# One inversion pass over 62 slots for two disjoint token lists, in place of two passes

## The chip, the cores and the metric

The kernel runs on one core of a Trainium2 chip. The metric is the device time of one execution, in microseconds; where there are several runs, their median.

## The reference, cut to what matters

A causal seven-tap convolution along the sequence is followed by two mixtures of eight experts. The first one is skipped by tokens whose skip score isn't positive, and adds its result to its input; the second one takes every token.

```python
def reference(x, weight, moe, moe2):
    x = conv(x, softmax(weight)).reshape(N, D)      # N = 14336, D = 192, F = 1024, E = 8
    do = x @ moe.w_skip > 0
    xc = x[do]
    e, gate = argmax(xc @ moe.w_gate), max(softmax(xc @ moe.w_gate))
    x[do] = xc + gate * (relu(xc @ moe.w1[e]) @ moe.w2[e])
    logits = x @ moe2.w_gate + moe2.modality_bias[modality_id]
    e, gate = argmax(logits), max(softmax(logits))
    return gate * (relu(x @ moe2.w1[e]) @ moe2.w2[e])
```

## The kernel before, in words

**Stages.** Phase 1 convolves all tokens in 8 groups of 16 columns of 112 tokens, computes the gates of both mixtures, and writes a row for each token to DRAM (`rows`). The tokens then go through the experts in *jobs*: a job is a list of up to 128 row numbers (one slot, 128 tokens) and one expert. `Ffn.run` goes over the jobs: it gathers a job's rows by an indirect DMA on GpSimd, transposes them by DMA, multiplies with w1 (`mm1`, two halves of 20 matmuls; relu on ScalarE into `hh`, remainder on VectorE into `hlo`), and one job later with w2 (`mm2`), whose result VectorE and ScalarE scale with `c`.

**Jobs in order.** 56 jobs of the first mixture from fixed slots (7 per expert), 6 jobs of the tokens that overflow these slots (list `l1`, `NS1` = 6), 56 jobs of the second mixture for tokens that skip the first (list `lb`, `NS2B` = 56, the first 54 as pairs with one expert), and 58 jobs of the second mixture for the others, whose codes the first mixture's results give (list `l2`). The two lists `l1` and `lb` are made while the first 56 jobs run.

**How a list is made.** `route` has two halves. The *placement* (`ranks` and what follows it) gives every token of the list a position: one-hot codes `rA`, a running count `rC` over 128x1024 elements, two small TensorE products on the counts `cnt`, slot bounds `se`, per-expert shifts (`rB`, `rC`; 16 instructions, only for the paired list), a masking and a sum to `pos` (128x128, zero for a token that isn't in the list). It also makes the table `tab` of experts per slot, from which the weight loads read, and `nrem`, the count of slots that didn't fit. The *inversion* (`qsl`, `invert`) turns positions into row numbers per slot. `qsl` splits `pos` into a place `q` and a slot `sl`. `invert` goes over the 128 token columns in 16 chunks of 8: VectorE compares an iota with `q` into `oa` (128x1024) and with `sl` into `ob` (128 x 8S), multiplies `ob` by the row number, and TensorE adds up 8 products of `oa` and `ob`, S columns each, in one PSUM bank. S is 6 for `l1` and 56 for `lb`. `finish` writes the row numbers as `idx` (for `l1`) and `idxB` (for `lb`).

**What sets the order.** The instructions of VectorE, ScalarE, TensorE and GpSimd run in the order in which the program issues them (`InOrder`, whose line 70 is the line of nearly every instruction in the profile). Side work is written as generators. `Tasks.tick` goes one step in each live generator, and `bg` ticks at four points of each job, so a generator's steps lie between the jobs' instructions; a `yield n` skips n ticks. `routes` is such a generator: it waits for the slots of phase 1 (`idxs`), then runs `route` for `l1`, and then `route` for `lb`. Beside it run the two weight-preparation lanes (`prep`: load an expert's weights, a Gram product on TensorE with `dg` and `ssq` on VectorE and a small product with `ones`, then splits into f16 parts on ScalarE, GpSimd and VectorE, and stores) and `scale2` on finished results (`mx`, `s`, `ef`). At job 56 `bg` drains all that is left of them.

**What waits for the lists.** `run` gathers a job up to four jobs ahead (five for a pair) if its list is `ready`, and `need` steps `routes` until the list is there when the job is two ahead. The weights of overflow and second-mixture jobs are loaded on SP's queue, up to nine jobs ahead, as soon as `tab` is there and their buffer (one of three) is free.

Of the kernel before, what the change touches and what calls it, by code (L numbers as in the profile page):

```python
# [7 lines left out]
F32 = mybir.dt.float32  # L8
# [4 lines left out]
ALU = mybir.AluOpType  # L13
# [11 lines left out]
NT = 128  # L25
# [17 lines left out]
NS1 = 6  # L43
NP2B, NS2B = 27, 56
# [70 lines left out]
class Moe:  # L115
# [258 lines left out]
    def route_a(self, g, code, pool, ob, res):  # L374
        nc = self.nc
        S = NSA
        acc = self.acc[0][:, (g % 2) * S:(g % 2) * S + S]
        if g == 0:
# [5 lines left out]
        def count(h):  # L384
            a, b = AB.pop(h)
            for t in range(8):
                nc.tensor.matmul(acc, a[:, :, t], b[:, :S, t], start=(h % 2 == 0 and t == 0), stop=(h % 2 == 1 and t == 7))

# [53 lines left out]
        for h in (2 * g, 2 * g + 1):  # L442
# [5 lines left out]
            yield 2  # L448
            nc.vector.tensor_tensor(b[:, :S], self.iq[:, :S], sl[:, u].unsqueeze(1).to_broadcast([128, S, 8]), ALU.is_equal)
            nc.vector.tensor_tensor(b[:, :S], b[:, :S], self.val[:, u].unsqueeze(1).to_broadcast([128, S, 8]), ALU.mult)  # L450
            yield 2
# [4 lines left out]
        yield 2  # L456
        t1 = pool.tile([128, S], F32, name="t1a")
        nc.vector.tensor_scalar(t1, acc, 0.0, 2048.0 * g, ALU.is_gt, ALU.mult)
# [104 lines left out]
        yield 1  # L563

    def route(self, code, nst, tag, pool, ob, res, base=0, lag=1, S=None, np=0, lp=None, val=None):
        nc = self.nc
        lp = lp or self.cp
        S = S or nst
        T = code.shape[-1]
        r = []  # L570
        for w in self.ranks(code, pool, 1, r):
# [39 lines left out]
            yield 1  # L611
        nc.vector.tensor_tensor(cum, cum, oh, ALU.mult)
        yield 1
        pos = pool.tile([128, T], F32, name="pos")
        nc.vector.tensor_reduce(pos, cum.rearrange("p c t -> p t c"), AX.X, ALU.add)
        yield 1
        q, sl = self.qsl(pos, pool)
        yield 1
        ef = ob.tile([128, S + 6], F32, name="esl", bufs=1)
        nc.vector.memset(ef[:, 0:6], -1.0)  # L620
# [7 lines left out]
        tab = lp.tile([128, S, 2], I32, name="tab" + tag)  # L628
# [11 lines left out]
            nc.vector.tensor_tensor(tab[:, :, 1], ef[:, 6:], ef[:, 3:S + 3], ALU.not_equal)  # L640
        nrem = res.get("nrem") or lp.tile([128, 1], I32, name="nrem" + tag)
        nc.vector.tensor_scalar(nrem, se[:, 1 if np else 0, 8:9], -float(nst), 0.0, ALU.add, ALU.max)
        res.update(tab=tab, nrem=nrem)
        yield 1
        for w in self.invert(S, q, sl, pool, ob, tag, res, lp, lag, base, val):
            yield w


class Phase1:
# [454 lines left out]
def build(tc, x, cw, m1w1, m1w2, mod, bias2, m2w1, m2w2, wgs, out):  # L1104
    with ExitStack() as ctx:
        m = Moe(tc, ctx)
        nc = m.nc
# [6 lines left out]
        rt = ctx.enter_context(tc.tile_pool(name="rt", bufs=1))  # L1114
        ob = m.oa = ctx.enter_context(tc.tile_pool(name="ob", bufs=4))
        pw = ctx.enter_context(tc.tile_pool(name="pw", bufs=2))
        pq = ctx.enter_context(tc.tile_pool(name="pq", bufs=4))
        la, ls, l1, lb, l2, lr = {}, {}, {}, {}, {}, {}
# [35 lines left out]
        def routes():  # L1154
            while "idx" not in ls:
                yield 1
            va = m.cp.tile([128, NSA], F32, name="va")
            ra["va"] = va
            k = 0
            while k < NSA:  # L1160
                c = order[k][0] * SB + order[k][1]
                n = 1
                while k + n < NSA and order[k + n][0] * SB + order[k + n][1] == c + n:
                    n += 1
                nc.gpsimd.tensor_copy(va[:, k:k + n], ls["va"][:, c:c + n])
                k += n
                yield 1
            for i in m.route(m.code[:, 0, :], NS1, "1", rt, ob, l1, lag=2):
                yield i
            for i in m.route(m.code[:, 1, :], NS2B, "B", rt, ob, lb, lag=2, np=NP2B):  # L1170
                yield i

        tk, tk2, tkw = Tasks(), Tasks(), Tasks()
# [29 lines left out]
        w = {}  # L1203

        def late_pools():
            st.close()
            m.py.append(m.py2)
            m.ph.append(m.ph3)
            px = ctx.enter_context(tc.tile_pool(name="px", bufs=1))
            w["x"] = px.tile([128, NC - XA, D], F32, name="x2s")  # L1210
            po = sp.enter_context(tc.tile_pool(name="po", bufs=1))
            pw2 = sp.enter_context(tc.tile_pool(name="pw2", bufs=2))
            w["pw2"] = pw2
            tkw.add(lane(1))
            o = po.tile([128, 4, F], F16, name="o1"), po.tile([128, W2C + 2], F16, name="o2")
            w["o"] = o
            tk.add(routes())
# [44 lines left out]
        n1, n2 = NC, NC + NS2B  # L1262
# [110 lines left out]
```

## Time and profile before

| | us |
|---|---|
| three runs, median (lowest to highest) | 1087.74 (1078.09 to 1090.42) |
| the profiled execution | 1090.2 |
| its span, first to last instruction | 1088.4 |
| TensorE busy | 983.2 (90%) |
| VectorE busy | 696.8 (64%) |
| ScalarE busy | 492.7 (45%) |
| GpSimd busy | 626.7 (58%) |
| mean granted clock | 0.935 |

In the profile PE is TensorE's matmuls, PEld its weight loads, DVE VectorE, ACT ScalarE, POOL GpSimd, and SP the queue that issues most DMAs. Busy shares are averages over stages with different limits; a matmul's own duration is longer than its distance to the next, since matmuls are pipelined. The granted clock is a share of full speed: 1.00 is 2.4 GHz, 0.50 is 1.2 GHz, and values between are means over a stretch with both. Most instructions are issued through a helper and show its line, L70, so they are told apart by the names of their tiles. The two lists are made between 233 and 519 us of the span.

### The profile page before, as it was taken

To read this page: it belongs to the slowest core of one execution; us is meant where nothing else is said; L and a number is where in the kernel's file an instruction comes from. 1 tells how busy PE (TensorE), PEld (TensorE's weight loads), DVE (VectorE), ACT (ScalarE), POOL (GpSimd) and SP (SyncE) were. 2 spreads that over 40 slices of the span, in tenths; PEclk is the share of its full clock that TensorE was granted. 3 is DMA by queue.
4 is the path that set the end of the run, shared out by engine and by line. 5 is a ranking of instruction groups with operands and counts; after the bars stand their busy time and mean duration, and the time that the engine had idled before them with its cause. 6 is when DMAs were issued, how large, how long until landed. Compare 5 with 4: busy or idle time off the path is not lost.

```text
span 1088.4 us, 27310 instructions
## 1 busy us (share of the span) xinstructions
PE 983.2 (90%) x10104; PEld 818.9 (75%) x10104; DVE 696.8 (64%) x1813; ACT 492.7 (45%) x903; POOL 626.7 (58%) x1110
## 2 busy tenths in 40 slices
PE   6788988899999779999889999999997999999993
PEld 4566767778888668888777777788786888888882
DVE  4386876679998889888446666667753444444441
ACT  3374643443755635455345555553233333334331
POOL 4054667777756836676437777774434555555531
PEclk9897765999999888999999999999999999999997
DMA  5666446675679737867963333443156332323330
GB/s 197 210 227 236 132 148 215 159 225 162 188 183 278 217 124 224 242 203 222 286 225 98 94 105 92 106 102 90 49 141 242 80 74 71 78 72 71 79 118 15
DMA packets 109134, 165.35 MB, mean 152 GB/s; under 512 B 80975, under 2 KB 86073, under 8 KB 103232
## 3 DMA queue, kind: packets, MB, share of 16 engines
q1 hardware_dynamic: 94368, 134.02, 39.6%
q0 software_dynamic: 13920, 28.87, 11.3%
q8 instruction: 81, 1.33, 0.5%
q10 hardware_dynamic: 704, 0.63, 0.2%
q14 instruction: 61, 0.50, 0.1%
HBM read 181.56 MB, written 58.42 MB: 220 GB/s over the span
## 4 chain that ended last, share of the span: by engine, by line
PE 57%; DVE 16%; DMA 8%; issue 5%; ACT 5%; POOL 5%; SPq 1%; POOLq 0%; ACTq 0%; DVEq 0%
PE bank L70 57%; DVE hlo L70 3%; DMA out_dram<-u,si 3%; DMA ws<-in_moe_w_dram 2%; DVE rC L70 1%; ACT ws L70 1%; DVE ob L70 1%; DVE o L70 1%; ACT hh L70 1%; DVE ws L70 1%; DMA w1b<-s1b 1%; DVE mx L70 1%; DMA gt<-rows,idx 1%; DVE oa L70 1%; DMA gt<-rows,idxB 1%
## 5 line engine op out<-in xcount | busy, mean ns | idle before, releaser
L70 PEld LDWEIGHTS <-w1b 128*128 128x128 f16 x4840 | 374.7, 100 | 54.4 <-issue 13.5
L70 PE MATMUL bank<-xp,w1b 128*128 128x256 f16 x2200 | 266.8, 275 | 9.4 <-DMA w1b<-s1b 4.6
L70 PEld LDWEIGHTS <-ws 128*128 128x128 f16 (+2 forms) x2208 | 192.7, 101 | 67.2 <-DMA ws<-in_moe_w_dram 9.6
L70 PE MATMUL bank<-w2b,ws 128*128 128x384 f16 x1760 | 237.3, 286 | 0.7 <-issue 0.7
L70 DVE SCALAR_TENSOR_TENSOR ws<-bank,ws 128x512 f16<-128x512 f32 x220 | 151.5, 690 | 126.7 <-ACT ws L70 106.6
L70 POOL DMA_INDIRECT out_dram<-u,si x114 | 115.6, 1014 | 188.5 <-DVE u L70 52.1
L70 ACT ACTIVATE ws<-bank 128x512 f16<-128x512 f32 x220 | 130.7, 597 | 118.7 <-PE bank L70 105.9
L70 PE MATMUL bank<-xt,w1b 128*128 128x128 f16 x2640 | 168.9, 224 | 9.1 <-DVE hlo L70 7.0
L70 PE MATMUL bank<-w2b,hh 128*128 128x384 f16 x528 | 142.1, 336 | 2.2 <-DMA w2b<-s2a 1.2
L70 PE MATMUL bank<-w2b,hlo 128*128 128x192 f16 x528 | 131.9, 251 | 0.0
L70 ACT ACTIVATE u<-bank,c 128x192 f32<-128x192 f32 x114 | 48.0, 421 | 156.0 <-PE bank L70 117.2
L70 DVE SCALAR_TENSOR_TENSOR hlo<-bank,hh 128x512 f16<-128x512 f32 x132 | 90.2, 685 | 42.3 <-ACT hh L70 39.0
L70 DVE SCALAR_TENSOR_TENSOR u<-bank,c,u 128x192 f32<-128x192 f32 x114 | 47.6, 418 | 103.3 <-ACT u L70 79.4
L70 ACT ACTIVATE hh<-bank 128x512 f16<-128x512 f32 x132 | 76.2, 593 | 41.6 <-PE bank L70 39.6
L70 ACT COPY xt<-bank 128x384 f16<-128x384 f16 (+1 forms) x110 | 64.0, 582 | 47.9 <-PE bank L70 46.1
L70 PEld LDWEIGHTS <-xt 128*112 128x112 f16 (+1 forms) x570 | 49.1, 138 | 39.9 <-issue 29.8
L70 PEld LDWEIGHTS <-hh 128*128 128x128 f16 x528 | 53.6, 102 | 32.0 <-issue 4.1
L70 POOL DMA_INDIRECT gt<-rows,idx x64 | 63.8, 996 | 11.3 <-issue 9.1
L70 PE MATMUL bank<-xg,band 128*112 128x384 f32 x128 | 63.9, 591 | 0.3 <-DVE s L70 0.3
L70 POOL TENSOR_TENSOR x2s<-x2s,xs 128x192 f32<-128x192 f32 x46 | 31.6, 687 | 54.8 <-DVE x2s L70 45.0
L70 POOL DMA_INDIRECT gt<-rows,idxB x56 | 56.1, 1002 | 12.0 <-issue 7.2
L70 PE MATMUL bank<-g,xt 128*112 128x34 f16 (+1 forms) x570 | 47.3, 199 | 12.0 <-DVE L L70 5.0
(249 smaller groups left out, 1447.4 us busy)
## 6 DMA issues: line engine op xcount, KB each, us to landing
w1b<-s1b SPq DMA_DIRECT2D x59, 1024.0 KB
w2b<-s2b SPq DMA_DIRECT2D x59, 768.5 KB
ws<-in_moe_w_dram SPq DMA_DIRECT2D x16, 768.0 KB
rows<-hl SPq DMA_DIRECT2D x8, 1386.0 KB
xg<-in_x_dram SPq DMA_DIRECT2D x7, 1536.0 KB
ws<-in_moe_w_dram SPq DMA_DIRECT2D x16, 512.0 KB
ws<-in_moe_w_dram SPq DMA_DIRECT2D x32, 256.0 KB
s1a<-w1b SPq DMA_DIRECT2D x8, 1024.0 KB
```

What stands on the lines that cost most here:

```text
L70: r = f(*args, **kw)
```

## The change

`route` is cut in two: `place` (placement, table and `nrem`) and the inversion behind it. The new `route2` places the first list, places the second list, and inverts both at once. A token is in at most one of the two lists, since a token that skips the first mixture isn't among its overflow, so the two position arrays are merged in one: `keep` is the first list's position where it lies within its 6 slots (else zero), and a token of the second list gets its own position plus 6 x 128 (`far` is that shift). One `qsl` and one `invert` over 62 slots follow, and the two lists are slices of the result (`idx1B`). `pos` gets two buffers. `route`, which makes the other lists, does what it did.

```diff
--- before.py
+++ after.py
@@ -563,9 +563,38 @@
         yield 1
 
     def route(self, code, nst, tag, pool, ob, res, base=0, lag=1, S=None, np=0, lp=None, val=None):
+        S = S or nst
+        for w in self.place(code, nst, tag, pool, ob, res, lag, S, np, lp):
+            yield w
+        q, sl = self.qsl(res["pos"], pool)
+        yield 1
+        for w in self.invert(S, q, sl, pool, ob, tag, res, lp, lag, base, val):
+            yield w
+
+    def route2(self, codes, nsts, tags, pool, ob, ress, np, lag):
+        nc = self.nc
+        (c1, cb), (n1, nb), (t1, tb), (r1, rb) = codes, nsts, tags, ress
+        for w in self.place(c1, n1, t1, pool, ob, r1, lag, n1):
+            yield w
+        keep = pool.tile([128, NT], F32, name="keep")
+        nc.vector.scalar_tensor_tensor(keep, r1["pos"], float(n1 * 128), r1["pos"], ALU.is_le, ALU.mult)
+        for w in self.place(cb, nb, tb, pool, ob, rb, lag, nb, np):
+            yield w
+        far = pool.tile([128, NT], F32, name="pos", bufs=2)
+        nc.vector.tensor_scalar(far, rb["pos"], 0.0, float(n1 * 128), ALU.is_gt, ALU.mult)
+        nc.vector.tensor_tensor(keep, keep, far, ALU.add)
+        nc.vector.tensor_tensor(keep, keep, rb["pos"], ALU.add)
+        q, sl = self.qsl(keep, pool)
+        yield 1
+        res = {}
+        for w in self.invert(n1 + nb, q, sl, pool, ob, t1 + tb, res, None, lag):
+            yield w
+        for r, a, b in ((r1, 0, n1), (rb, n1, n1 + nb)):
+            r.update(idx=res["idx"][:, a:b], va=res["va"][:, a:b])
+
+    def place(self, code, nst, tag, pool, ob, res, lag, S, np=0, lp=None):
         nc = self.nc
         lp = lp or self.cp
-        S = S or nst
         T = code.shape[-1]
         r = []
         for w in self.ranks(code, pool, 1, r):
@@ -611,10 +640,8 @@
             yield 1
         nc.vector.tensor_tensor(cum, cum, oh, ALU.mult)
         yield 1
-        pos = pool.tile([128, T], F32, name="pos")
+        pos = pool.tile([128, T], F32, name="pos", bufs=2)
         nc.vector.tensor_reduce(pos, cum.rearrange("p c t -> p t c"), AX.X, ALU.add)
-        yield 1
-        q, sl = self.qsl(pos, pool)
         yield 1
         ef = ob.tile([128, S + 6], F32, name="esl", bufs=1)
         nc.vector.memset(ef[:, 0:6], -1.0)
@@ -640,10 +667,8 @@
             nc.vector.tensor_tensor(tab[:, :, 1], ef[:, 6:], ef[:, 3:S + 3], ALU.not_equal)
         nrem = res.get("nrem") or lp.tile([128, 1], I32, name="nrem" + tag)
         nc.vector.tensor_scalar(nrem, se[:, 1 if np else 0, 8:9], -float(nst), 0.0, ALU.add, ALU.max)
-        res.update(tab=tab, nrem=nrem)
-        yield 1
-        for w in self.invert(S, q, sl, pool, ob, tag, res, lp, lag, base, val):
-            yield w
+        res.update(tab=tab, nrem=nrem, pos=pos)
+        yield 1
 
 
 class Phase1:
@@ -1165,9 +1190,7 @@
                 nc.gpsimd.tensor_copy(va[:, k:k + n], ls["va"][:, c:c + n])
                 k += n
                 yield 1
-            for i in m.route(m.code[:, 0, :], NS1, "1", rt, ob, l1, lag=2):
-                yield i
-            for i in m.route(m.code[:, 1, :], NS2B, "B", rt, ob, lb, lag=2, np=NP2B):
+            for i in m.route2((m.code[:, 0, :], m.code[:, 1, :]), (NS1, NS2B), ("1", "B"), rt, ob, (l1, lb), NP2B, 2):
                 yield i
 
         tk, tk2, tkw = Tasks(), Tasks(), Tasks()
```

VectorE, in the first jobs behind the first placement. Ahead of the change; `oa` and `ob` are the first chunks of the six-slot pass, `hlo`, `c` and `x2a` belong to jobs, `dg` and `ssq` to weight preparation:

```order
L70 SCALAR_TENSOR_TENSOR hlo<-bank_59,hh 128x512
L70 TENSOR_SCALAR esl<-esl 128x6
L70 CAST tab_3803<-esl 128x6
L70 TENSOR_TENSOR tab_3803<-esl 128x6
L70 TENSOR_SCALAR nrem_3807<-se 128x1
L70 TENSOR_TENSOR c<-gt,w2b_79 128x1
L70 TENSOR_TENSOR oa<-iq,q 128x1024
L70 SCALAR_TENSOR_TENSOR x2a<-bank_64,c,x2a 128x192
L70 TENSOR_TENSOR ob<-iq,sl 128x48
L70 SCALAR_TENSOR_TENSOR hlo<-bank_63,hh 128x512
L70 SCALAR_TENSOR_TENSOR hlo<-bank_58,hh 128x512
L70 TENSOR_TENSOR ob<-ob,val 128x48
```

And in the changed program, at the same place:

```order
L70 CAST tab_3770<-esl 128x6
L70 TENSOR_TENSOR tab_3770<-esl 128x6
L70 TENSOR_SCALAR nrem_3774<-se 128x1
L70 SCALAR_TENSOR_TENSOR hlo<-bank_59,hh 128x512
L70 SCALAR_TENSOR_TENSOR keep<-pos 128x128
L70 TENSOR_TENSOR rA<-code,c_205 128x1024
L70 TENSOR_TENSOR c<-gt,w2b_79 128x1
L70 SCALAR_TENSOR_TENSOR rC<-rA 128x1024
L70 MEMSET gend 128x1
L70 COPY gend<-rC 128x8
L70 TENSOR_TENSOR cnt<-gend 128x8
L70 SCALAR_TENSOR_TENSOR x2a<-bank_64,c,x2a 128x192
```

Where the first chunks stood, the second list's placement begins (`rA`, the scan `rC`, `gend`, `cnt`).

VectorE in the changed program, at the end of the second placement (`pos` on the left of the third row is `far`, `x2s` and `mx` belong to jobs):

```order
L70 TENSOR_SCALAR nremB<-se 128x1
L70 TENSOR_REDUCE mx<-x2a 128x4
L70 SCALAR_TENSOR_TENSOR x2s<-bank_60,c,x2s 128x192
L70 TENSOR_SCALAR pos<-pos 128x128
L70 TENSOR_TENSOR keep<-keep,pos 128x128 x2
L70 TENSOR_SCALAR pi<-keep 128x128
L70 TENSOR_SCALAR si<-pi 128x128
L70 TENSOR_SCALAR sl<-si 128x128
L70 TENSOR_SCALAR pi<-pi 128x128
```

The merging stands there, and one `qsl` behind it; in the program before each placement had a `qsl` of its own.

VectorE at the end of the second list's inversion, before the change (`c`, written once per job, has been written 56 times there):

```order
L70 TENSOR_TENSOR rC<-rC,bank_61 128x224
L70 SCALAR_TENSOR_TENSOR x2s<-bank_64,c,x2s 128x192
L70 TENSOR_REDUCE ei_8542<-rC 128x56
L70 TENSOR_TENSOR ei<-ei,ei_8542 128x56
L70 TENSOR_SCALAR vaB<-ei 128x56
L70 TENSOR_SCALAR idxB<-ei 128x56
L70 SCALAR_TENSOR_TENSOR hlo<-bank_58,hh 128x512
```

And at the end of the joint inversion in the changed program (`c` has been written 36 times):

```order
L70 SCALAR_TENSOR_TENSOR hlo<-bank_58,hh 128x512
L70 TENSOR_REDUCE ei_6489<-rC 128x62
L70 TENSOR_TENSOR ei<-ei,ei_6489 128x62
L70 TENSOR_SCALAR va1B<-ei 128x62
L70 TENSOR_SCALAR idx1B<-ei 128x62
L70 TENSOR_SCALAR wsc<-bank_65 128x2
L70 TENSOR_SCALAR wsc<-wsc 128x2 x2
```

The end of the list work has moved ahead by 20 jobs; the list that the overflow jobs read is written there too, where it was written after 31 jobs.

## Rows read from the trace of the kernel before

**Rows 1.** Busy time by stretch of the list work; number of instructions in brackets.

```profile
core 0: us, PE busy (x) PEld busy (x) DVE busy (x) ACT busy (x) POOL busy (x), PEclk, DMA share, GB/s
233.10:259.20 26.10, 24.63 (x332) 21.26 (x331) 22.88 (x48) 11.28 (x18) 21.60 (x30) 1.00 0.67 218
259.20:287.40 28.20, 27.02 (x373) 23.86 (x370) 25.60 (x71) 17.00 (x29) 18.96 (x28) 1.00 0.39 98
259.20:367.60 108.40, 102.19 (x1388) 89.89 (x1386) 96.22 (x239) 66.72 (x118) 74.37 (x108) 1.00 0.70 195
367.60:409.50 41.90, 29.01 (x323) 24.83 (x322) 35.62 (x88) 16.23 (x30) 22.18 (x31) 0.81 0.55 160
409.50:516.40 106.90, 104.64 (x1313) 92.57 (x1312) 93.43 (x216) 59.22 (x106) 74.53 (x107) 0.98 0.74 224
516.40:547.00 30.60, 23.41 (x286) 20.16 (x284) 12.83 (x33) 9.79 (x20) 14.36 (x28) 0.94 0.98 267
```

**Rows 2.** The same stretches, instructions that touch `c` alone; ACT's count is jobs.

```profile
233.10:259.20 26.10, 4.18 (x10) 1.68 (x4) 0.00 (x0) 1.00 0.67 218
259.20:287.40 28.20, 3.64 (x13) 2.52 (x6) 0.00 (x0) 1.00 0.39 98
259.20:367.60 108.40, 12.81 (x41) 8.35 (x20) 0.00 (x0) 1.00 0.70 195
367.60:409.50 41.90, 4.40 (x12) 2.08 (x5) 0.00 (x0) 0.81 0.55 160
409.50:516.40 106.90, 11.98 (x40) 8.34 (x20) 0.00 (x0) 0.98 0.74 224
516.40:547.00 30.60, 3.90 (x12) 2.50 (x6) 0.00 (x0) 0.94 0.98 267
```

**Rows 3.** TensorE in order of time: start, duration; a chunk of each inversion, and what follows.

```profile
268.12 0.61 PE L70 MATMUL bank<-ob,oa 128*128 128x6 f16 x8
268.59 0.32 PE L70 MATMUL bank<-w2b,hh 128*128 128x384 f16 x1
...
500.98 1.02 PE L70 MATMUL bank<-ob,oa 128*128 128x56 f16 x8
501.83 0.34 PE L70 MATMUL bank<-w2b,hh 128*128 128x384 f16 x1
```

**Rows 4.** TensorE: the first matmuls of two jobs without list work between them.

```profile
512.08 2.40 PE L70 MATMUL bank<-xt,w1b 128*128 128x128 f16 x40
...
516.27 2.40 PE L70 MATMUL bank<-xt,w1b 128*128 128x128 f16 x40
```

**Rows 5.** Stretches again: instructions that touch `oa`, then those that touch `ob`.

```profile
259.20:367.60 108.40, 9.80 (x128) 9.50 (x128) 11.72 (x16) 1.00 0.70 195
...
259.20:367.60 108.40, 9.80 (x128) 14.08 (x32) 1.00 0.70 195
...
409.50:516.40 106.90, 16.42 (x128) 16.54 (x32) 0.98 0.74 224
```

**Rows 6.** What TensorE waited for from 367.6 to 409.5: us, times, longest.

```profile
PE bank L70 <- DVE ssq L70: 6.8, 1, 6.8
PE bank L70 <- DVE cnt L70: 3.2, 1, 3.2
PE bank L70 <- DVE hlo L70: 2.6, 1, 2.6
```

**Rows 7.** TensorE in two stretches of 5 us of the second placement.

```profile
370.00:375.00 5.00, 1.28 (x20) 0.83 1.06 266
375.00:380.00 5.00, 3.84 (x25) 0.50 0.75 210
```

**Rows 8.** GpSimd in order of time: the gather that waits for the second list.

```profile
518.83 0.94 POOL L70 DMA_INDIRECT gt<-rows,idxB  x1 [3.09 <-DVE idxB L70]
```

**Rows 9.** VectorE in order of time: instructions on 128x128 elements.

```profile
259.27 0.23 DVE L70 TENSOR_SCALAR pi<-pos 128x128 int32<-128x128 f32 x1
...
394.96 0.35 DVE L70 SCALAR_TENSOR_TENSOR rC<-rC,sb,rB 128x128 f32<-128x128 f32 x1
```

## The prediction, made before the change was run

> **What bounds the kernel now.** I read the page's slices first (TensorE 9 of 10 almost everywhere), then the chain that ended last (57% TensorE), then the stretch in which the two lists are made, cut at the jobs. [rows 1] is that cut: placement of the first list (233.1 to 259.2), its inversion (to 367.6), placement of the second list (to 409.5), its inversion (to 516.4), and the stretch behind it, in which the weights of the overflow jobs are loaded. [rows 2] counts the jobs in each: ScalarE scales each job's second half by `c` once, so the ACT count is 4, 20, 5, 20 and 6 jobs. The paces follow: 26.1/4 = 6.5 us for a job, 108.4/20 = 5.42, 41.9/5 = 8.38, 106.9/20 = 5.35. A job without any list work needs 4.19 us of TensorE (start of one `mm1` half to the next, 516.27 - 512.08) [rows 4]; weight preparation adds its own matmuls to some of them.
>
> In both inversions TensorE is the bound: 102.2 of 108.4 us and 104.6 of 106.9 us busy [rows 1]. In the placement of the second list it is not: TensorE is busy 29.0 of 41.9 us at a mean granted clock of 0.81, and waits 6.8 us for `ssq`, 3.2 us for `cnt` and 2.6 us for `hlo`, all VectorE [rows 6]. The clock falls with that: it is 0.83 in the 5 us in which TensorE is busy for 1.28 us and 0.50 in the next five [rows 7], that is, its lower level of 1.2 GHz. So there are two prices: an inversion costs TensorE time, a placement costs VectorE time and then clock.
>
> **The change part by part.**
>
> *The six-slot inversion goes.* It is 16 chunks of 8 matmuls (and 8 weight loads of `oa`) on TensorE. One chunk delays the next matmul by 268.59 - 268.12 = 0.47 us [rows 3]; 16 x 0.47 = 7.5 us. On VectorE it is 16 `oa` and 32 `ob` instructions, 11.7 + 14.1 = 25.8 us of busy time [rows 5], more than TensorE's share, but beside TensorE's work in a stretch that TensorE bounds.
>
> *The remaining pass gets 62 columns for 56.* A chunk of 56 takes 501.83 - 500.98 = 0.85 us [rows 3]. 50 columns more than six cost 0.38 us, so six more cost about 0.05 us, 16 x 0.05 = 0.7 us. On VectorE each `ob` grows by 48 elements: the 32 `ob` instructions take 16.5 us at 448 elements and 14.1 at 48 [rows 5], so less than 1 us in all.
>
> The Trainium skill, TensorE: Matmul & The Clock Gate, section Back-to-back issue gap, lets 1 to 64 columns cost the same, about 25 ns. By it the widening would be free and the whole narrow pass 128 x 25 ns = 3.2 us, an estimate from that page, so this part would bring about 3.6 us less than the rows say. The rows differ: 59 ns a matmul at 6 columns, 106 ns at 56 [rows 3], and I keep the rows.
>
> *The merging of positions.* `keep`, `far` and two additions are four VectorE instructions on 128x128. The nearest rows of that size are 0.35 us (a scalar_tensor_tensor) and 0.23 us (`pi`, a tensor_scalar) [rows 9]: 3 x 0.35 + 0.23 = 1.3 us. One `qsl` of five such instructions goes, 5 x 0.23 = 1.2 us. Net nothing; were a port shared with GpSimd to hold each of them as it holds some `ob`, it would be a few us of VectorE at most, and the order puts them beside `hlo`, where TensorE has a job of lead.
>
> *What moves.* The order shows that the second placement now follows the first at once, in the jobs where the first chunks of the six-slot pass stood, and that the joint inversion ends 20 jobs ahead of where `idxB` is written now. Nothing is moved past a DMA: SP's queue keeps its order. So the old stages (4 jobs placement, 20 inversion, 5 placement, 20 inversion) become: 4 jobs placement, 6 jobs placement, 19 jobs inversion, 20 jobs with no list work. I price each.
>
> 1. First placement: as now, 26.1 us.
> 2. Second placement, now in the jobs that take 28.2 us today [rows 1]. VectorE in the first inversion: 96.2 - 25.8 = 70.4 us for 20 jobs that isn't list work, 3.5 us a job. So the second placement itself is 35.6 - 5 x 3.5 = 18.1 us of VectorE [rows 1, 2], and here the stage needs 18.1 + 6 x 3.5 = 39.1 us of VectorE, against 28.2 us that six jobs with chunks take today. I take 39. The ends: 28.2 if TensorE's lead of a job and the absent chunks cover it all, and 6 x 8.38 = 50.3 if it costs per job what it costs today, waits and low clock included.
> 3. Joint inversion over 19 jobs: the first inversion's pace, which has the same preparation work beside it, with the wider chunks: (108.4 + 16 x (0.85 + 0.05 - 0.47)) x 19/20 = 109.5 us.
> 4. The last 20 jobs: 106.9 - 16 x 0.85 = 93.3 us.
>
> Sum: 26.1 + 39 + 109.5 + 93.3 = 267.9 us against 26.1 + 108.4 + 41.9 + 106.9 = 283.3: 15.4 us less. Of this 6.8 us is matmul time (7.5 - 0.7); the rest is TensorE's wait and low clock in the second placement, and VectorE waits in the first inversion, of which a part goes.
>
> *The wait for `idxB`.* GpSimd's gather for the first pair job stands 3.1 us at 518.83 because `idxB` is written only just before [rows 8]. With the list ready 20 jobs earlier this wait goes. What is late next is DMA: in 516.4 to 547 the share is 0.98 at 267 GB/s, and TensorE is busy for 23.4 of 30.6 us [rows 1]. The gather comes earlier into queues that are full. I take 0, with ends of 0 and 3.1 us of gain. The overflow jobs' list (`idx`) is written later than now but, by the order, about 16 jobs before its first gather: no wait is added.
>
> The sum stands against the profiled execution, 1090.2 us (span 1088.4 and 1.8 around it): 1074.8. That execution is 2.5 us above the median of the runs, 1087.74, so I predict 1072.
>
> **The rivals.** What a measurement of this kernel can tell from no change is about 1%, here 10.9 us: below 1076.9 is faster.
>
> *A. The second placement keeps its price per job* (50.3 us in step 2). The gain is 15.4 - 11.3 = 4 us: 1084, no change. For it: VectorE is already busy 22.9 of 26.1 us in the first placement, and the second now follows with no lighter job between. Against: the 6.8 us wait for `ssq` hung on where a preparation step fell among the placement's large instructions; in the new place the order has the one `ssq` of these jobs right behind `cnt`, ahead of most of them.
>
> *B. The placement is covered* (28.2 us). The gain is 15.4 + 10.8 = 26 us: 1061. For it: the six jobs lose about five chunks of the narrow pass, 5/16 x 25.8 = 8 us of VectorE. Against: 18.1 us come.
>
> *C. The last 20 jobs meet the DMA.* They move 224 GB/s over 106.9 us now, 23.9 MB [rows 1]. At the 267 GB/s of the next stretch that is 89.7 us, just below the 93.3 of step 4. Should loads and stores come in lumps, the stage could take 100 us: a gain of 9 us, 1079.
>
> *D. Slower: the clock.* VectorE, filled by two placements in a row, never catches up in the joint inversion; TensorE waits before each chunk and runs there at the mean clock of the placement, 0.81 [rows 1]. Step 3 is then 109.5/0.81 = 135.2 us, 25.7 more, the result 10.3 us slower: 1098. It decides from a mean clock of about 0.88 in that stage (109.5/0.876 is 15.4 us more). Against: in the present first inversion VectorE is busy 96.2 of 108.4 us and the clock stays at 1.00 [rows 1].
>
> The Trainium skill's same page, section Why this matters for your kernels, warns that idle gaps between bursts of matmuls bring back the lower rate. The trace agrees with the direction in the placement, where the clock goes to 0.50 behind waits [rows 7]; in the inversions, with shorter waits, no row shows it.
>
> **How the numbers follow.** Forecast (12 to 19 us gained) 0.50, A 0.20, B 0.15, C 0.10, D 0.05. Faster by over 1%: the forecast but for its lowest part, and B, 0.60; slower, D, 0.05; the rest, 0.35, within 1%. The range goes from B (1061, with the gather's 3.1 us partly on top) to A with 2 us for the runs' spread: 1060 to 1086.
>
> **What would show it.** In the profile after: 128 matmuls with 128x62 in this stretch and none with 128x6; the joint list (`idx1B`) written some 20 jobs before the first overflow job's half; six jobs of second placement in about 39 us, with some low clock; 20 jobs at about 4.7 us behind it; GpSimd no longer waiting for the list. I am wrong if the second placement takes near 50 us or near 28, if the joint inversion shows a clock below 1.00 for long, or if the last 20 jobs show TensorE waiting for loads.

## The result, and the profile after

| | before | after |
|---|---|---|
| median of 22 runs each (lowest to highest), us | 1087.0 (1078.1 to 1093.3) | 1093.3 (1084.0 to 1100.1) |
| ratio, 95% interval | | 1.0068 (1.0049 to 1.0088) |
| profiled span, us | 1088.4 | 1091.7 |

The change costs 6.3 us where 15 less were forecast: the prediction was wrong, in its sign and in its range. The page of the changed kernel begins:

```profile
PE 974.5 (89%) x9976; PEld 808.6 (74%) x9976; DVE 683.4 (63%) x1755; ACT 493.0 (45%) x903; POOL 623.1 (57%) x1110
```

The 128 matmuls of the narrow pass are gone (10104 before, 9976 now), and TensorE is busy for 8.7 us less. The work shrank; the time grew. To see where, I cut every trace at the same instruction, VectorE's addition of a job's result (`x2a`, `x2s`), counted in jobs from the first: the first placement begins in job 7, the second now in job 11, the last chunk ends in job 36, and in job 56 the fixed slots end. Below are the changed kernel's four stretches (jobs 7 to 11, 11 to 17, 17 to 36, 36 to 56; columns as in [rows 1]).

```profile
230.22:255.88 25.66, 24.18 (x328) 20.87 (x326) 22.25 (x46) 11.29 (x19) 19.60 (x24) 1.00 0.65 202
255.88:301.35 45.47, 31.86 (x370) 26.54 (x369) 43.76 (x100) 20.34 (x34) 26.16 (x34) 0.92 0.39 107
301.35:420.10 118.75, 108.48 (x1338) 96.99 (x1338) 100.91 (x228) 63.37 (x114) 71.62 (x101) 0.94 0.68 188
420.10:520.14 100.04, 92.50 (x1182) 79.62 (x1181) 67.97 (x157) 59.59 (x106) 70.27 (x111) 0.97 0.83 242
```

The stages of before, cut in this way, come within 0.3 us of the forecast's stretches [rows 1]: 26.1, 108.3 (jobs 11 to 31), 41.7 and 106.8, in all 282.9 us. After they sum to 289.9. These 7.0 us are about as much as the median lost. By stretch:

| us | jobs 7-11 | 11-36 | 36-56 | 7-56 |
|---|---|---|---|---|
| before | 26.1 | 149.9 | 106.8 | 282.9 |
| forecast for after | 26.1 | 148.5 | 93.3 | 267.9 |
| after | 25.7 | 164.2 | 100.0 | 289.9 |

In the second placement VectorE is busy for 43.8 of 45.5 us, and the clock is not at 1.00 in any of the three later stretches. TensorE's waits in jobs 11 to 17, 17 to 36 and 36 to 56 (columns as in [rows 6]):

```profile
PE bank L70 <- DVE hlo L70: 8.0, 3, 3.5
PE bank L70 <- DVE cnt L70: 2.5, 1, 2.5
...
PE bank L70 <- DVE hlo L70: 9.1, 2, 7.8
PE bank L70 <- DVE ob L70: 3.7, 3, 1.6
...
PE bank L70 <- DVE ssq L70: 3.2, 1, 3.2
PE bank L70 <- DMA xt<-gt: 2.4, 3, 1.0
```

In the kernel before, jobs 11 to 36:

```profile
PE bank L70 <- DVE ssq L70: 7.4, 2, 6.8
PE bank L70 <- DVE hlo L70: 5.0, 4, 2.6
```

The `ssq` wait of 6.8 us [rows 6] is gone, as the forecast had it, but `hlo` takes 17.1 us in these 25 jobs for 5.0 before. A job's second product needs `hlo`, and `hlo` reads the bank of its first product, so later first products wait for it too. The longest wait, 7.8 us, is of that kind and stands at the end of the second placement. VectorE there, in order of time:

```profile
296.73 0.20 DVE L70 TENSOR_TENSOR esl<-esl,e 128x56 f32<-128x56 f32 x1
...
298.06 2.45 DVE L70 TENSOR_TENSOR tabB<-esl 128x54 int32<-128x54 f32 x2
...
301.92 0.97 DVE L70 TENSOR_TENSOR keep<-keep,pos 128x128 f32<-128x128 f32 x2
302.93 0.76 DVE L70 TENSOR_SCALAR pi<-keep 128x128 int32<-128x128 f32 x1
...
304.54 0.23 DVE L70 CAST q<-pi 128x128 f16<-128x128 int32 x1
305.24 0.68 DVE L70 SCALAR_TENSOR_TENSOR hlo<-bank,hh 128x512 f16<-128x512 f32 x1
```

And TensorE behind it, then, apart, two of its stretches of 5 us there (columns as in [rows 7]):

```profile
305.97 2.29 PE L70 MATMUL bank<-xt,w1b 128*128 128x128 f16 x20 [7.77 <-DVE hlo L70]
```

```profile
300.00:305.00 5.00, 0.00 (x0) 0.74 0.88 214
305.00:310.00 5.00, 4.03 (x39) 0.58 0.09 20
```

Slot table, merging and `qsl` run for 8 us (296.7 to 304.8) ahead of the `hlo` that TensorE needs, with 1.3 us of a finished job's `mx` and `x2s` between them. Some 2.2 us of it is one of the two `tabB` instructions: the pair takes 2.45 us here and 0.29 in the kernel before, and it ends with a subtraction on GpSimd (300.4 us; below on such holds):

```profile
416.56 0.29 DVE L70 TENSOR_TENSOR tabB<-esl 128x54 int32<-128x54 f32 x2
```

```profile
298.73 1.63 POOL L70 TENSOR_TENSOR w2b<-ws,w2b 128x768 f16<-128x768 f32 x1
```

TensorE does nothing from 300 to 305, and its clock is 0.58, close to its lower level of 1.2 GHz, in the next five.

### The profile page after: what moved, and what is told of

The parts are those of the page before. It is cut to its first block, busy times and chain, and to the rows that moved or that the text cites. A ratio compares the mean times of both kernels' runs of the same rounds, so it can differ in the third digit from the quotient of the medians.

```text
span 1091.7 us, 26993 instructions
## 1 busy us (share of the span) xinstructions
PE 974.5 (89%) x9976; PEld 808.6 (74%) x9976; DVE 683.4 (63%) x1755; ACT 493.0 (45%) x903; POOL 623.1 (57%) x1110
## 5 line engine op out<-in xcount | busy, mean ns | idle before, releaser
L70 PE MATMUL bank<-xp,w1b 128*128 128x256 f16 x2200 | 264.0, 274 | 3.7 <-DMA xp<-gt 1.9
L70 PE MATMUL bank<-xt,w1b 128*128 128x128 f16 x2640 | 172.6, 227 | 22.1 <-DVE hlo L70 14.7
L70 PE MATMUL bank<-w2b,hh 128*128 128x384 f16 x528 | 145.8, 343 | 6.8 <-DMA w2b<-s2a 4.2
L70 PE MATMUL bank<-w2b,hlo 128*128 128x192 f16 x528 | 134.6, 256 | 3.7 <-DVE hlo L70 3.7
L70 ACT ACTIVATE hh<-bank 128x512 f16<-128x512 f32 x132 | 76.7, 594 | 51.3 <-PE bank L70 49.6
L70 PEld LDWEIGHTS <-xt 128*112 128x112 f16 (+1 forms) x570 | 46.7, 132 | 38.5 <-issue 27.3
L70 POOL DMA_INDIRECT gt<-rows,idx1B x62 | 61.9, 998 | 10.0 <-issue 7.4
L70 POOL DMA_INDIRECT gt<-rows,idx x58 | 57.5, 991 | 10.3 <-issue 8.7
L70 PEld LDWEIGHTS <-hlo 128*128 128x128 f16 x528 | 53.9, 102 | 12.2 <-issue 7.3
```

Source lines behind the costliest of these rows:

```text
L70: r = f(*args, **kw)
```

## The experiments

Each ratio is against the kernel before, run beside it on the same chip (its median there was 1077.3 to 1086.7 us). Whole-kernel ratios have intervals of some 0.4% either way, so I read the runs by the cut above. Two executions say how sharp it is.

**Repeats, no edit.** 

> The program before once more, for a second profile: it shows how far a stage's time repeats. If the stages repeat, the stretch of 49 jobs with the list work takes 282.9 us as in the first profile, within 1 us, and only what lies ahead of it (it began at 234 us) moves by some us. If they don't, the comparison of stages between two single profiles says little.

> The changed program once more: 289.9 us for the same 49 jobs within 1 us if stages repeat, with a stall of TensorE behind the store of prepared weights in jobs 46 to 51 (29.7 us); elsewhere, if that stall was a chance of this one execution.

Measured: 282.6 and 289.7 us for jobs 7 to 56 (282.9 and 289.9 the first time). The whole executions were 1071.1 and 1096.0 us. So in these two kernels the stretch repeats within 0.3 us, and its parts within 1 us, while the whole of one kernel moves by 19. The spread kernel below repeats less well: 281.8 and 284.0 us, and its jobs 11 to 36 take 149.9 and 146.7. A difference of less than some 3 us that rests on one trace is therefore not firm.

**The move alone.** The changed order of placements, with both inversions kept apart.

```diff
         for w in self.place(c1, n1, t1, pool, ob, r1, lag, n1):
             yield w
...
+        q1, s1 = self.qsl(r1["pos"], pool, "1")
+        yield 1
         for w in self.place(cb, nb, tb, pool, ob, rb, lag, nb, np):
             yield w
...
+        qb, sb = self.qsl(rb["pos"], pool)
+        yield 1
+        for w in self.invert(n1, q1, s1, pool, ob, t1, r1, None, lag):
+            yield w
+        for w in self.invert(nb, qb, sb, pool, ob, tb, rb, None, lag):
+            yield w
```

> The program before with one thing moved: both placements stand first, then the two inversions of 6 and of 56 slots, each as before. Theory P (the second placement costs more right behind the first one, in jobs with more VectorE work): the changed program lost 7 us although 6.8 us of matmul time left it, so this one should be 12 to 16 us slower than before, 1099 to 1103, with the second placement at about 41 us and low clock behind it. Theory M (the move is harmless; the merging, the 62 columns or the faster jobs behind cost): within 3 us of before, 1084 to 1090. Theory F (only the last jobs without list work lose, on stores and loads): also within 3 us, since here the last 20 jobs carry an inversion.

Measured: jobs 7 to 56 289.9 us, ratio 1.0029 (0.9986 to 1.0071). With the same work as before, the move alone costs 7.0 us of the stretch, in jobs 11 to 36 (158.0 us for 149.9). The whole kernel, slower by 3.1 us in the middle of its interval and 7.7 at most, falls short of the 12 to 16 that theory P expected. Against this kernel the changed one takes 6.2 us more in jobs 11 to 36, where its chunks are wider (16 x 0.45 = 7.2), and 6.1 us less in jobs 36 to 56 (100.0 for 106.1), where 13.6 us of chunks are gone. So 7.5 of those 13.6 us don't come out: what the narrow pass should bring is lost in the last 20 jobs.

**What the narrow pass is worth.** In the kernel before, the first list's `invert` is replaced by a pause of 77 ticks (`skip`), and in a second kernel the second list's is. The list is written empty there.

```diff
+        if skip:
+            yield 77
+            ei = ob.tile([128, S], F32, name="ei", bufs=1)
+            nc.vector.memset(ei, 0.0)
+            self.finish(tag, ei, S, res, base, lp)
...
         for w in self.invert(S, q, sl, pool, ob, tag, res, lp, lag, base, val):
```

> The program before without the 16 chunks of the six-slot inversion; its ticks pass empty and its list is written empty, so the overflow slots compute on a row of zeros. It gives the worth of that pass where it stood. P: its matmul time and a part of the waits, 7 to 13 us faster than before, 1074 to 1080. Rival (the pass was hidden, or the jobs only run into the loads): within 3 us, 1084 to 1090.

> The program before without the 16 chunks of the second inversion; its ticks pass empty and its list is written empty, so the pair jobs gather one row of zeros and only the jobs up to 56 can be compared. F (something other than list work bounds jobs 36 to 56 at 5 us a job): 99 to 101 us there. If only the changed program's stalls did it: 106.8 - 13.6 = 93 us, as the prediction had it.

Measured: without the narrow pass jobs 11 to 31 take 101.1 us for 108.3, 7.2 less (forecast 7.5), and the kernel 0.9948 (0.9909 to 0.9987). Without the wide pass jobs 36 to 56 take 95.8 for 106.8: 11.1 of the 13.6 us of matmuls come out, which lies between the two expectations; its one execution was 1070.4 us beside a median of 1077.3 for the kernel before on that chip.

**The wide pass at 62 columns, in the kernel before.**

```diff
-        for w in self.invert(S, q, sl, pool, ob, tag, res, lp, lag, base, val):
+        wd = {}
+        for w in self.invert(S + (NS1 if tag == "B" else 0), q, sl, pool, ob, tag, wd, lp, lag, base, val):
             yield w
+        res.update(idx=wd["idx"][:, 0:S], va=wd["va"][:, 0:S])
```

> The program before with only one thing: the second list's inversion is 62 columns wide, six of them unused, its place unchanged. By the sum of the prediction the 16 chunks cost 0.7 us of TensorE more: jobs 36 to 56 take 107 to 108 us against 106.8 of the program before, no change in time. Rival (the widening itself costs, by more than its matmul time): 110 us or more in those jobs, as the late-placed version had 30.7, 29.6, 27.7 us for jobs 36 to 51 where the program before has 28.6, 27.2, 27.5.

Measured: jobs 36 to 56 take 108.6 us for 106.8, 1.8 more (forecast 0.7; one trace); ratio 1.0023 (0.998 to 1.0065).

**The second placement later.** One line ahead of it in the changed kernel, with 60, 30, 72 and 10 ticks (four ticks are a job):

```diff
+        yield 60
         for w in self.place(cb, nb, tb, pool, ob, rb, lag, nb, np):
```

> The changed program, with the second placement 60 ticks (15 jobs) later, so that it stands about where it stood before, and the joint inversion behind it, ending five jobs ahead of the drain. P: the placement costs what it cost before, and the six-slot pass is gone: 7 to 12 us faster than before, 1075 to 1080. M: the merged pass itself costs, so it stays at the changed program's 1093. F: the jobs without list work now stand ahead of the placement, in a stretch with as many loads and stores; between 1083 and 1093.

> The changed program with the second placement 30 ticks (7.5 jobs) later, so between the changed program and the version with 60 ticks. If what the first placement leaves behind on VectorE is what makes the second dear (theory P1), the placement costs there what it costs at 60 ticks, and jobs 11 to 36 take some 147 us (145 at 60 ticks, 164 at none), 1087 to 1090 in all. If the price hangs on which preparation steps the large instructions meet (theory P2), it can lie anywhere between 145 and 164 us.

> The changed program with the second placement 72 ticks (18 jobs) later, three jobs later than at 60 ticks; the list is done just ahead of its first gather. P1: jobs 7 to 56 as at 60 ticks, 279 to 281 us, 1087 to 1090. P2: different by several us either way. If the list comes late for the gathers, the jobs from 51 on take longer.

> The changed program with the second placement 10 ticks (2.5 jobs) later. If the excess is VectorE's backlog from the first placement, it is gone: jobs 11 to 36 take 156 to 158 us (164 in the changed program, of which 1.6 us less of chunks stand in these jobs). If it is the meeting with preparation steps, they can take 160 or more. In all 1087 to 1091.

A late placement pushes chunks out of jobs 11 to 36, so I price the placement alone: the stretch less 0.92 us for each chunk in it (matmuls that touch `oa`, over 8) and less 25 jobs at 101.1/20 = 5.05 us, the pace of the run without the narrow pass.

| ticks late | jobs 11-36 | chunks in it | placement | ratio to before |
|---|---|---|---|---|
| before (narrow chunks, 0.47 us) | 149.9 | 16 | 16.1 | |
| 0 (after) | 164.2 | 16 | 23.2 | 1.0068 (1.0049 to 1.0088) |
| 10 | 159.1 | 15.6 | 18.4 | 1.0073 (1.0032 to 1.0115) |
| 30 | 153.0 | 10 | 17.5 | 1.0012 (0.9976 to 1.0047) |
| 60 | 145.1 | 3 | 16.0 | 1.0028 (0.9991 to 1.0065) |
| 72 | 144.8 | 0 | 18.5 | 0.9988 (0.9936 to 1.004) |

By this working the placement costs 16 to 18.5 us in each of these places and 5 to 7 more directly behind the first. Other traces agree: directly behind the first it is 22.9 us in the repeat of the changed kernel and 24.2 in the move alone (narrow chunks), and in the old place 14.9 in the kernel without the narrow pass. As times of the whole kernel the expectations failed all the same: none of the four is clearly faster than before, and at 60 ticks 7 to 12 us were expected. At 72 ticks the stretch 7 to 56 is 283.0 us, that of before: the list is then late, and GpSimd's gather waits 6.36 us for `idx1B`.

**The second placement stretched threefold**, in place of a pause.

```diff
         for w in self.place(cb, nb, tb, pool, ob, rb, lag, nb, np):
-            yield w
+            yield 3 * w
```

> The changed program with the second placement's steps three times as far apart: it spreads over about 17 jobs in place of 6, so VectorE has 18.1/17 = 1.1 us of it per job besides 3.5 us. P: the waits for it and the low clock go, 15 to 20 us less than the changed program, 1073 to 1078. M: stays at 1093. F: the loss in the last jobs stays, 1083 to 1088.

> The changed program with the second placement spread, once more, since its first profile (281.8 us for the 49 jobs, 1.1 less than before) doesn't fit its time (0.6% above before). If the stage's time repeats, the median comes near 1086. If it doesn't, the median stays near 1094 and this profile shows a longer stage than the first, and where.

Measured: jobs 7 to 56 281.8 and 284.0 us, ratios 1.0063 (1.0025 to 1.0101) and 1.0058 (1.0011 to 1.0105). The 15 to 20 us less that theory P expected didn't come. The stretch is about as long as before; the kernel isn't, and the traces show from job 56 to the first output store 50.2 and 51.3 us (46.4 before). By the working above, with 7 chunks in jobs 11 to 36, the placement costs 17.2 and 14.0 us: spreading isn't shown to make it cheaper than a pause does.

**The chunks two ticks later**, once alone and once with the pause of 30.

```diff
         q, sl = self.qsl(keep, pool)
+        yield 2
```

> The changed program with the joint inversion two ticks (half a job) later and nothing else: it moves every chunk to other points of the jobs and of the preparation. If only sums count (VectorE's work per job), jobs 17 to 51 take what they take in the changed program, 198 us, within 1 us. If they hang on which steps fall together (P2), they move by 3 us or more.

> The changed program with the second placement 30 ticks later and the chunks two ticks later. If what each brought adds up: jobs 7 to 56 at 276 to 277 us against 282.9 before, and 3 to 5 us faster than before, 1080 to 1083. If the points at which chunks meet the preparation were luck in each: within 3 us of the 30-tick version, 1084 to 1088, not to be told from before.

Measured: 286.0 us alone (3.9 less than after; ratio 1.0051, 1.0014 to 1.0087), 281.6 with the pause (278.9 without the two ticks; ratio 1.0013, 0.9979 to 1.0047). Two ticks alone bring jobs 17 to 51 from 198.3 to 193.2 us, where the expectation by sums allowed 1 us; together with the pause the two gains don't add up. How the list work falls among the preparation's steps may move the stretch by some us in either direction, but each of these is one trace.

**The weight stores exchanged**, for the stall in jobs 46 to 51 (below).

```diff
-            nc.sync.dma_start(ws[q][2][e], o1)
-            yield 2 + q
             nc.sync.dma_start(ws[q][3][e], o2.bitcast(I32))
             yield 2 + q
+            nc.sync.dma_start(ws[q][2][e], o1)
+            yield 2 + q
```

> The changed program with the two stores of a prepared expert exchanged: the part that is overwritten first by the next expert is stored first, three ticks sooner. Theory F (in the last 20 jobs, without chunks, the jobs run into the store: VectorE stood 3.6 us for it, TensorE 3.2 us behind VectorE, and the clock fell): jobs 46 to 51 take 24 to 25 us in place of 29.7, and the whole 4 to 6 us less than the changed program, 1087 to 1089. Theory P (only the placement and what stands behind it costs): unchanged, 1093.

Measured: jobs 7 to 56 290.4 us, jobs 46 to 51 28.6 (24 to 25 expected if the order of the stores were the cause), ratio 1.0062 (1.0023 to 1.0102). VectorE's wait for the store of `o` (`s2b`) is gone, and ScalarE has it, for the other one:

```profile
480.92 1.05 ACT L70 CAST o<-ws 128x1024 f16<-128x1024 f32 x1 [4.57 <-DMA s1b<-o]
```

**GpSimd's large subtractions in quarters**, in the changed kernel and in the one before.

```diff
-            nc.gpsimd.tensor_tensor(o1[:, 1, :], wt, o1[:, 0, :], ALU.subtract)
+            for k in range(0, F, F // 4):
+                nc.gpsimd.tensor_tensor(o1[:, 1, k:k + F // 4], wt[:, k:k + F // 4], o1[:, 0, k:k + F // 4], ALU.subtract)
...
-            nc.gpsimd.tensor_tensor(o2v[:, 0:4, D:], w2v[:, 0:4], o2v[:, 0:4, 0:D], ALU.subtract)
+            for k in range(4):
+                nc.gpsimd.tensor_tensor(o2v[:, k:k + 1, D:], w2v[:, k:k + 1], o2v[:, k:k + 1, 0:D], ALU.subtract)
```

> After, with each of GpSimd's two subtractions of weight preparation (128x1024 and 128x768) issued in four quarters; nothing else differs. In the profile of after seven VectorE instructions of jobs 11 to 36 take over 1 us longer than their shortest like (11.7 us in all; four and 5.0 us in before), each beside such a subtraction. If a GpSimd subtraction holds VectorE and TensorE pays for it: these instructions lose most of the 11.7 us (a hold of at most 0.6 us is left), and jobs 11 to 36 take 158 to 161 us instead of 164.2, jobs 7 to 56 284 to 287 instead of 289.9. If the excess behind the first placement is VectorE's own backlog: the holds go or stay, but jobs 11 to 36 stay at 163 to 165 us.

> Before, with the same quarters. If holds by GpSimd explain why after is dearer in jobs 11 to 36, they cost little here, where only four instructions show them: jobs 11 to 36 take 148 to 150 us (149.9 before), jobs 7 to 56 281 to 283 (282.9), the whole kernel the same within 0.3 percent. If the quarters themselves cost or bring something (more GpSimd instructions, an earlier start of VectorE's part), before moves by as much as after does.

Jobs 11 to 17, 17 to 36 and 36 to 56 of the changed kernel with quarters:

```profile
256.06:297.89 41.83, 31.76 (x357) 26.56 (x356) 40.12 (x101) 20.31 (x34) 25.51 (x40) 0.88 0.36 100
297.89:417.21 119.32, 109.62 (x1354) 97.53 (x1352) 100.23 (x229) 63.72 (x114) 77.41 (x135) 0.96 0.66 192
417.21:513.44 96.23, 89.45 (x1185) 77.44 (x1182) 68.19 (x157) 59.34 (x106) 74.51 (x138) 1.00 0.88 252
```

Seven held instructions became two (11.7 us over their shortest like became 3.6), and jobs 11 to 36 take 161.1 us for 164.2. In the kernel before the quarters leave that stretch at 149.7 (149.9; jobs 36 to 56 take 2.4 us more). Both theories had other numbers: 161.1 lies between the 158 to 161 of one and the 163 to 165 of the other. Holds may be worth about 3 us of the 7 here, by one trace and no more than the spread kernel's repeat moves. As a cure the quarters fail: 1.0121 (1.0083 to 1.0158) in the changed kernel, 1.0036 (0.9997 to 1.0075) in the one before. The profiled execution, 1089.7 us, was the fastest of the changed kernel's five, so its trace doesn't show where the others lose.

**Where the cut should end.** Jobs 51 to 56 gain 2.5 to 3.0 us wherever the list is early (20.5 to 21.0 for 23.5). But from job 51 to the first output store those kernels take 65.8 to 71.8 us, for 70.0 and 69.1 before, so most of them give the gain back, and the stretch 7 to 56 flatters them. From job 7 to the first output store the traces show, in us:

| kernel | job 7 to the first output store |
|---|---|
| before, two executions | 329.3, 328.2 |
| after, two executions | 336.8, 338.8 |
| move alone | 339.1 |
| second placement 10, 30, 60, 72 ticks later | 334.0, 327.3, 329.5, 328.5 |
| spread, two executions | 332.0, 335.3 |
| chunks two ticks later; with the pause of 30 | 331.4; 329.1 |
| stores exchanged | 340.0 |
| quarters in the changed kernel | 333.9 |

Cut there, each difference to before lies within a whole-kernel interval or less than 1 us outside it, but for two: the move alone (10 us more, where its ratio allows 7.7) and the quarters in the changed kernel (5 us more, where theirs asks for 9). Those two stay open.

No kernel with the complete work is shown to beat the one before.

## Why the prediction was wrong, step by step

**The pass itself: right.** The narrow pass was put at 7.5 us and its removal, in the kernel before, brought 7.2. A chunk of 62 columns was put at 0.90 us; here it is 384.38 - 383.46 = 0.92:

```profile
383.46 1.10 PE L70 MATMUL bank<-ob,oa 128*128 128x62 f16 x8
384.38 0.80 PE L70 MATMUL bank<-xt,w1b 128*128 128x128 f16 x11
```

The Trainium skill, TensorE: Matmul & The Clock Gate, section Back-to-back issue gap, which the forecast weighed, has 1 to 64 columns cost the same for a matmul by itself, and says that this counts too little where each matmul comes with a weight load. That is the case here, so the forecast's 3.2 us for the narrow pass used the figure where the page doesn't claim it. The measured 0.92 us a chunk of 62 columns against 0.47 of six shows that columns count for these matmuls.

**Step 2 and the start of step 3: the step that failed.** The forecast took a placement as 18.1 us of VectorE, of which TensorE's lead would hide a part: 39 + 109.5 us for the 25 jobs, which leaves 148.5 - 16 x 0.90 - 25 x 5.05 = 7.8 us for it. It cost 23.2, so the overlap with TensorE that was taken off its price wasn't there. Three things were missed.

- *Its price was never 8.* By the same working it cost 16.1 us in the old place, and 16.0 to 18.5 in four later ones. So in each of these places a placement costs most of its VectorE time. The traces fit that VectorE, in order, has `hlo`, `dg` or `ssq` queued behind the placement while TensorE waits for them: which of them is late changes with the place (in jobs 11 to 36 `ssq` 7.4 us before, `hlo` 16.7 at 60 ticks, `dg` 8.6 at 72), and the price only by 2.5 us. The forecast priced the old place by its waits and low clock, and took those as mishaps that a move would leave behind. One of them (`ssq`) did stay behind; `hlo` took its place.
- *The cut was early.* I took the 18.1 us from a stretch that ends at 409.5 us, ahead of the slot table and `nrem`. At the new place table, merging and `qsl` are in the 8 us shown above, of which some 2.2 are a hold and 1.3 a job's own. Step 2's VectorE load is not far off (43.8 us busy for 39.1), but the piece behind it falls in step 3, which takes 118.7 us for 109.5. Its other stretch of low clock (0.61 and 0.70 from 390 to 400 us) stands beside two waits of 1.3 and 1.4 us for `hlo` and `ob`.
- *Two placements in a row cost more.* Ten ticks between them bring the price from 23.2 to 18.4; that VectorE had no time to catch up fits this, but isn't shown. The two runs that bear on the cause of this excess each bring it down in part: quarters to 20.1 and two ticks before the chunks to 20.3, each by one trace. Holds by GpSimd and the meeting with preparation steps may both have a share; how they divide with a plain backlog stays open.

**Step 4: mis-sized.** The last 20 jobs were put at 93.3 and take 100.0. The step took all 13.6 us of the chunks out; even in the kernel before only 11.1 come out (95.8). Most of the other 4.2 us stands at one stall, which comes again at the same place in the repeat (jobs 46 to 51: 29.7 and 29.6 us, 26.4 without the second pass, 24.5 with the quarters). VectorE and TensorE in order of time, then TensorE's clock behind:

```profile
476.89 0.15 DVE L70 TENSOR_SCALAR o<-kf 128x1 int32<-128x1 int32 x1 [3.58 <-DMA s2b<-o]
...
483.74 0.59 PE L70 MATMUL bank<-ssq,ones 128*128 128x2 f32 x2 [3.17 <-DVE ssq L70]
```

```profile
485.00:490.00 5.00, 5.00 (x30) 0.50 0.76 243
```

With the jobs faster, preparation reaches its next expert while the store of the last one is still under way; `o` has one buffer, so VectorE stands, TensorE waits 3.17 us for `ssq` behind it, and the next 5 us run at 0.50. In the kernel before without the second pass the same wait is there, nearly as long, and the clock stays at 1.00:

```profile
473.18 0.38 PE L70 MATMUL bank<-ssq,ones 128*128 128x2 f32 x2 [2.89 <-DVE ssq L70]
```

```profile
475.00:480.00 5.00, 5.00 (x65) 1.00 0.87 291
```

So the wait comes with jobs that have no chunks, and what the changed kernel adds is the low clock: 0.89 over jobs 46 to 51. The exchange of the stores shows that their order isn't the cause: the wait moves to ScalarE, and TensorE's wait for `ssq` stays (3.63 us). That leaves the single buffer, which no run doubled. Rival C had this size (100 us) by lumps of DMA; what is seen is one store and one buffer.

**The wait for `idxB`: right that it goes and brings nothing.** The gathers of the six overflow jobs read slices of the same list now; the line below is the gather for the first pair job, right behind the last of them. It no longer waits for the list:

```profile
519.34 0.95 POOL L70 DMA_INDIRECT gt<-rows,idx1B  x1 [0.30 <-issue]
```

Jobs 51 to 56 gain 3.0 us (20.5 for 23.5), and from job 51 to the first output store it is 67.4 and 69.7 us, for 70.0 and 69.1 before. TensorE's waits behind job 56, to the first output store, are for loads, as the forecast's "what is late next" had it:

```profile
PE bank L70 <- DMA w2b<-s2a: 4.2, 3, 3.7
PE bank L70 <- DMA xt<-gt: 2.8, 1, 2.8
```

**The rivals.** The result lies past A (the placement keeps its price per job), and A, C and part of D happened together: D's low clock is there (0.94 in step 3), but from a few waits, the longest (7.8 us) at its start, and not ahead of each chunk. I gave the three chances as if one of them would come alone. The sign was lost there: with the placement at 16 us in any place and C's 100 us, the sum is 26.1 + 126.3 + 16 + 14.4 + 100 = 282.8, no change at all, before any excess.

## What to carry to other kernels

In this kernel side work on an in-order engine that also feeds the bound engine cost most of its own duration in each of the places tried, and two such pieces in a row cost more than apart. So price such work by the same stage with and without it, to its last instruction, and do not count its waits as bad luck of the place. Work taken off the bound engine brings only what the next resource lets through: of 13.6 us of matmuls 11.1 came out, and a stall behind a store took part of the rest. And end a cut behind the next thing that waits, or it counts a gain that is given back.

## What the runs showed of the hardware

**VectorE held beside GpSimd.** VectorE and GpSimd in the changed kernel, in order of time:

```profile
273.31 2.27 DVE L70 SCALAR_TENSOR_TENSOR rC<-rC,sb,rB 128x128 f32<-128x128 f32 x1
...
385.40 2.11 DVE L70 SCALAR_TENSOR_TENSOR kf<-wsc 128x1 f32<-128x1 f32 x1
...
473.16 0.15 DVE L70 SCALAR_TENSOR_TENSOR kf<-wsc 128x1 f32<-128x1 f32 x1
...
273.31 2.13 POOL L70 TENSOR_TENSOR o<-ws,o 128x1024 f16<-128x1024 f32 x1 [4.62 <-ACT o L70]
...
385.37 2.13 POOL L70 TENSOR_TENSOR w1b<-ws,w1b 128x1024 f16<-128x1024 f32 x1 [1.64 <-ACT w1b L70]
```

The first takes 0.35 us elsewhere [rows 9], the second, of one element per partition and with both inputs in `wsc`, 0.15. Each started within 0.03 us of a GpSimd subtraction of 2.13 us and lasted about as long. The Trainium skill, GPSIMD Engine Reference, section Key points, says that GpSimd shares its SBUF interfaces with VectorE and that instructions with two SBUF inputs contend; the trace agrees, and shows that even a one-element instruction can be held for all of the other's time.

**The scatter lies elsewhere.** Job 7 begins at 223.4 to 236.2 us in the traces of this case, though nothing ahead of it was edited but in the two kernels with quarters (229.6 and 229.7 us) and the one with exchanged stores (231.8). Behind the first output store the two executions of the kernel before take 524.8 and 517.6 us. The 49 jobs from job 7 on repeat within 0.3 us in the kernels before and after, and within 2.2 in the spread one. A stage cut at the same instruction can tell what the medians of whole runs can't, if it is repeated.
